# A finished token tile's layer norm recorded one step later, in a fused attention and feed-forward kernel

## The chip, the cores and the metric

The kernel runs on one core of a Trainium2 chip. The metric is the device time of one execution in microseconds (us). A profile of one further execution, taken by the hardware profiler, shows what every engine did: TensorE (PE, with its weight loads PEld), VectorE (DVE), ScalarE (ACT), GpSimd (POOL) and SyncE (SP, which here only issues transfers).

## The reference

Four batches, eight heads, 1152 positions of 64 elements. Queries are averaged in pairs of positions, so there are 576 rows of queries for each head. Attention is followed by a layer norm and a two-layer feed-forward part with a residual.

```python
q_pool = q.reshape(B, H, S // factor, factor, D).mean(axis=3)
scores = scale * np.matmul(q_pool, k.transpose(0, 1, 3, 2))
scores = scores - np.max(scores, axis=-1, keepdims=True)
attn = np.exp(scores)
attn = attn / (np.sum(attn, axis=-1, keepdims=True) + 1e-09)
attn_out = np.matmul(attn, v)
x = attn_out.transpose(0, 2, 1, 3).reshape(B, S, H * D)   # 4 x 576 x 512
xn = (x - mu) / np.sqrt(var + 1e-06) * g_ln
out = x + np.maximum(xn @ w_ch1, 0.0) @ w_ch2              # 512 -> 2048 -> 512
```

## The kernel before

**Steps.** A pair p is one batch and two heads; there are 16 pairs, and each has nine chunks of 128 query rows, so 144 steps. Step i takes the chunk i % 9 of pair i // 9 through a software pipeline that is written out by hand in `step(i)`. No scheduler reorders anything: each engine executes its instructions in the order in which the functions record them, and waits for the others by semaphores. In a step of batches 1 to 3 the order of recording is:

- VectorE's maximum of the scores (`emit_max`, L381) and the bias from it (L386);
- TensorE's scores of the next step (`emit_s(i + 1)`, L362 and L370), into one of two slots of three PSUM banks;
- `flush()`: the evacuations that were put off, on ScalarE and VectorE (`r` L513 and L514; kt and qt L286 and L283; ht L629 and L630; xn and xh L577 and L578);
- ScalarE's exp (L395, into a tile pe, two buffers) and the high half (`emit_hi`, L409, into hl, three buffers);
- `final`: ScalarE's evacuations L524 of the attention output into the token tile xb or xh, and behind each `evacuated(n)`, which counts how many chunks of the tile are there;
- the low half of step i - 1 (`emit_lo`): on VectorE as L418, or, in steps whose chunk is 2, 5 or 8, on GpSimd as L251 and L416; then SyncE's transposing transfer of hl into pt;
- `norm(i)`, at most one a step;
- the scales of the next pair (L232 to L242), when due;
- TensorE: attention times v (`a_piece`, L464), transposes of raw k or q (`a_prep`), one unit of the feed-forward part (`some_units`, L616 or L648), in an order that depends on whether transposes of a norm follow;
- what was booked for this step with `at(i, ...)`: among it the conversions of v on GpSimd (`take_v`, L251, L251, L278) and the transposes of a normalized tile (`ln_t`, L571).

Batch 0 runs in another form (`on_pe`), in which P is transposed on TensorE and VectorE evacuates the output.

**A norm.** A token tile is 128 tokens by 512, and it is whole when eight chunks have been evacuated into it. Then `evacuated` appends it to `norms`. `norm(i)` takes the first of them: `ln_a` records VectorE's statistics (L553, L554); `ln_r` records three small GpSimd operations (L559, L562, L563) and the normalization L565 into xs, on GpSimd while attention runs and on VectorE after. The four transposes of xs (L571, TensorE) are booked for step i + 2, or i + 1 once the steps of attention are over, and the feed-forward units for the step behind. A batch b has tiles (b, 0) to (b, 3); the fifth chunk of every pair makes half a tile, and two batches share such a half tile, h.

**PSUM.** Outside the two slots only banks 6 and 7 are free while attention runs. `bank()` hands them out in turn; a transposing group or a unit can only start when what was last in its bank has been evacuated by ScalarE and then VectorE.

Of the kernel before, what the change touches and what calls it, by code (L numbers as in the profile page):

```python
# [24 lines left out]
def tile_pooled_attention_moe(  # L25
# [23 lines left out]
    C = S // 128  # L49
    HP = H // 2  # L50
    NP = B * HP
    NSTEP = NP * C
# [44 lines left out]
    def drip(n=1):  # L97
        while n and (soon or fill):
            (soon or fill).popleft()()
            n -= 1  # L100
# [235 lines left out]
    def on_pe(i):  # L336

        return 0 <= i < HP * C
# [38 lines left out]
    def emit_max(i):  # L377
        st = steps[i]
        mx = sm_p.tile([128, 1], FP32, tag="mx", name="mx")
        nb = st["nb"] = sm_p.tile([128, 1], FP32, tag="nb", name="nb")  # L380
        nc.vector.tensor_reduce(mx, st["s"], axis=AX.X, op=ALU.max)  # L381
        sc = pair[i // C]["sc"]
        if on_pe(i):
            st["mx"] = mx
        else:
            nc.vector.tensor_scalar(nb, mx, sc[:, 0:1], -1.0, op0=ALU.mult, op1=ALU.mult)  # L386
# [44 lines left out]
    def emit_t_copy(i):  # L431
        st = steps[i]
        for a, b in ((0, 512), (512, S)):
            nc.scalar.copy(st["pt"][:, a:b], st["s"][:, a:b])
# [115 lines left out]
    def ln_a(st, x):  # L550
        bs = sm_p.tile([128, 6], FP32, tag="bs", name="bs")
        mv = sm_p.tile([128, 2], FP32, tag="mv", name="mv", bufs=5)
        nc.vector.bn_stats(bs, x)  # L553
        nc.vector.bn_aggr(mv, bs)  # L554
        st["x"], st["mv"] = x, mv

    def ln_r(st, eng):
        rs = sm_p.tile([128, 2], FP32, tag="rs", name="rs", bufs=2)
        nc.gpsimd.tensor_scalar(  # L559
            rs[:, 1:2], st["mv"][:, 1:2], 1e-6, 2.0 ** -4, op0=ALU.add, op1=ALU.mult  # L560
        )
        nc.gpsimd.tensor_scalar(rs[:, 0:1], st["mv"][:, 0:1], -1.0, 1.0, op0=ALU.mult, op1=ALU.mult)  # L562
        nc.gpsimd.tensor_tensor(rs[:, 1:2], rs[:, 1:2], nhalf, op=ALU.pow)  # L563
        xs = st["xs"] = x_p.tile([128, DM], FP32, tag="xs", name="xs")
        eng.tensor_scalar(xs, st["x"], rs[:, 0:1], rs[:, 1:2], op0=ALU.add, op1=ALU.mult)  # L565

    def ln_t(st, dst):

        ps = bank()
        for c in range(KD):  # L570
            nc.tensor.transpose(  # L571
                ps[:, 128 * c:128 * c + 128], st["xs"][:, 128 * c:128 * c + 128], ident
            )
        pv = ps.rearrange("p (c n) -> p c n", c=KD)
        hi, lo = dst[:, 0:KD], dst[:, KD:2 * KD]
        return (
            lambda: nc.scalar.copy(hi, pv),  # L577
            lambda: nc.vector.tensor_tensor(lo, pv, hi, op=ALU.subtract),  # L578
        )
# [5 lines left out]
    def until(fns, n=None):  # L585
        evacs.extend((n, fn) for fn in fns)
# [213 lines left out]
    def at(i, fn, *a):  # L800
        todo.setdefault(i, []).append((fn, a))
# [52 lines left out]
    this = [0]  # L854
# [10 lines left out]
                at(i0 + x, fn, 4 * part + n)  # L865


    norms, turns = deque(), set()
    room = {"xn": 2, "x": 8}
    batch = {}  # L870

# [24 lines left out]
    def norm(i):  # L896

        if not norms or norms[0][1] % 2 == 0 and norms[0][0] != "h" and not room["xn"]:
            return
        b, t = norms.popleft()  # L900
        st = {}
        if b == "h":
            x = xh[t][:, 0]
            dst = xh[t][:, 1].bitcast(FP16).rearrange("p (a n) -> p a n", a=2 * KD)
        else:
            x = xb[b][:, t]
            keep = batch.setdefault(b, {})
            if t % 2 == 0:
                keep["xn", t] = x_p.tile([128, 2 * KD, 256], FP16, tag="xn", name="xn")
                room["xn"] -= 1  # L910
            dst = keep["xn", t - t % 2][:, :, 128 * (t % 2):128 * (t % 2) + 128]
        ln_a(st, x)
        ln_r(st, nc.gpsimd if i < NSTEP else nc.vector)

        def transpose():
            until(ln_t(st, dst), nbank[1])

        d = 2 if i < NSTEP else 1
        at(i + d, transpose)
        turns.add(i + d)  # L920
        if b == "h":
            at(i + d + 1, units_of_half, t)
        elif t % 2:
            at(i + d + 1, units_of, b, t)
            if t == 3 and b == 1:
                at(i + d + 1, lambda: norms.append(("h", 0)))
# [3 lines left out]
    def evacuated(n):  # L930

        p, j = divmod(n, C)
        b = p // HP
        left[p] -= 1
        if not left[p]:
            pair.pop(p)
        key = ("h", b // 2) if j == 4 else (b, PLACES[p % HP // 2][j][1])
        whole[key] = whole.get(key, 0) + 1
        if whole[key] == 8 and key != ("h", 0):
            norms.append(key)  # L940

    left = [C] * NP
    ready = {}
# [4 lines left out]
    def a_prep():  # L948
        if preps:
            fn, p, u = preps.popleft()  # L950
            until(fn(p, u), nbank[1])
# [6 lines left out]
    def a_piece(i):  # L958
        pieces.extend(ready.pop(i, ()))
        for u in range(2 if len(pieces) > 2 and not on_pe(i) else 1):  # L960
            if pieces:
                n = pieces.popleft()
                pt = pts[n]
                ps = emit_pv(n, bank() if u or on_pe(n) else None)
                if on_pe(n):
                    ot = pt.rearrange("p a n -> p (a n)").bitcast(FP32)[0:65, 0:128]
                    until([lambda ot=ot, ps=ps: nc.scalar.activation(
                        out=ot, in_=ps[0:65, 0:128], func=ACTF.Identity, bias=eps
                    )], nbank[1])
                    turned.append((n, ot))  # L970
                    continue
                one, two = evac_pv(n, ps)
                until([one], nbank[1] if u else None)
                last.extend((two, lambda n=n: evacuated(n)))

    def step(i):
        live = i < NSTEP
        this[0] = i
        for fn, a in early.pop(i, ()):
            fn(*a)  # L980
        if live:
            emit_max(i)
        if on_pe(i - 1):
            emit_t_copy(i - 1)
            steps.pop(i - 1)
        while found:
            found.popleft()()
        first = on_pe(i - 2) or on_pe(i)
        final, last[:] = list(last), []
        if first and not on_pe(i):  # L990
            a_piece(i)
        if on_pe(i):
            if i < 3:
                warm(16, bank())
            a_piece(i)
            a_prep()
            emit_exp(i)
        while scaled_out:
            scaled_out.popleft()()
        if i + 1 < NSTEP:  # L1000
            emit_s(i + 1)
            pv_slot[0] = i + 1
        else:
            free_banks[:] = [6, 7, 0, 1, 3, 4]
            pv_slot[0] += 1
        if on_pe(i):
            while fill:
                drip()
            flush()
        else:  # L1010
            flush()
            if live:
                emit_exp(i)
                emit_hi(i)
        for fn in final:
            fn()
        if 0 <= i - 1 < NSTEP and not on_pe(i - 1):
            emit_lo(i - 1)
            steps.pop(i - 1)
            drip()  # L1020
        norm(i)
        red = None
        while soon or len(fill) > 3:
            drip()
        if on_pe(i):
            emit_t(i)
            if reds:
                found.append(reds.popleft()())
        elif reds:
            red = reds.popleft()  # L1030
            put = [None]
            until([lambda: put[0]()])
        while turned:
            n, ot = turned.popleft()
            emit_turn(n, ot, i)
        if not on_pe(i):
            if not first:
                a_piece(i)
            if red:
                put[0] = red()  # L1040
            if i in turns:
                a_prep()
            some_units(i)
            if i not in turns:
                a_prep()
        for fn, a in todo.pop(i, ()):
            fn(*a)
        if calm and i < HP * C - 1:
            gate()
        for _ in range(1 if i < HP * C - 1 else 2):  # L1050
            if calm:
                fn, n = calm.popleft()
                fn(n)

    def warm(n, ps=None):
        ps = psum[:, 2, 0:128] if ps is None else ps[:, 0:128]
        for _ in range(n):
            nc.tensor.matmul(out=ps, lhsT=ident16, rhs=ident16, start=True, stop=True)

    with tc.manual_schedule():  # L1060
# [47 lines left out]
        i = 0  # L1108
# [32 lines left out]
```

## Time and profile before

| | before |
|---|---|
| median of 3 runs | 849.92 us (846.39 to 850.97) |
| profiled execution, its own time | 847.87 us |
| its span, first to last instruction | 846.1 us |
| TensorE busy | 812.0 us (96%) |
| VectorE busy | 599.8 us (71%) |
| ScalarE busy | 557.6 us (66%) |
| GpSimd busy | 351.4 us (42%) |
| mean granted TensorE clock | 0.989 |

The busy share of an engine is an average over all stages. Idle time of an engine is put down to the event that ended it; it costs something only where the work that waited is itself waited for, in the end by the engine that ends last. The granted clock is 1 at 2.4 GHz and 0.5 at 1.2 GHz.

### The profile page before, as it was taken

What the parts mean: (1) busy time and instruction counts of PE and PEld (TensorE: products, weight loads), DVE (VectorE), ACT (ScalarE), POOL (GpSimd) and SP (SyncE); (2) the same over time, 40 slices, a digit from 0 to 9 for tenths busy, and PEclk for the clock granted to TensorE, in tenths of its full rate; (3) what the DMA queues carried; (4) which work ended last, traced back from release to release, by engine and by line L of the source; (5) the groups of instructions that cost most, each with busy time, mean ns of one, the idle gap of its engine ahead of it and who ended that gap; (6) DMA issues with size and microseconds to landing.
All of it is one profiled execution on the core that took longest, in us unless ns stands there. A gap on an engine that the chain in (4) does not pass through costs nothing.

```text
span 846.1 us, 21643 instructions
## 1 busy us (share of the span) xinstructions
PE 812.0 (96%) x9142; PEld 577.8 (68%) x9142; DVE 599.8 (71%) x1166; ACT 557.6 (66%) x810; POOL 351.4 (42%) x345
## 2 busy tenths in 40 slices
PE   8999999988989999998999999999999999999997
PEld 6787878766656675656675766676766767766764
DVE  3698989887857888787787877878787877522221
ACT  3999998876666776786686868686778676311110
POOL 3020234395997964546434244635543422300000
PEclk9999999999999999999999999999999999999999
DMA  6853475024697879888899989787979777501001
GB/s 164 242 184 134 151 206 174 12 60 85 130 205 119 181 133 218 167 174 145 146 195 164 174 151 211 146 154 144 214 145 189 136 133 119 110 2 26 14 1 25
DMA packets 276018, 115.96 MB, mean 137 GB/s; under 512 B 259281, under 2 KB 259281, under 8 KB 275921
## 3 DMA queue, kind: packets, MB, share of 16 engines
q1 hardware_dynamic: 275568, 113.70, 65.8%
q8 instruction: 71, 1.16, 0.6%
q10 hardware_dynamic: 352, 0.88, 0.4%
q14 instruction: 27, 0.21, 0.1%
HBM read 46.14 MB, written 4.72 MB: 60 GB/s over the span
## 4 chain that ended last, share of the span: by engine, by line
PE 57%; DVE 12%; ACT 11%; DMA 9%; issue 5%; POOL 3%; SPq 2%; ACTq 0%; POOLq 0%; DVEq 0%
PE psum L648 17%; PE psum L616 17%; PE psum L464 7%; PE psum L362 6%; DMA pt<-hl 5%; ACT pe L395 4%; DVE mx L381 3%; PE psum L452 2%; PE psum L370 2%; DMA kr<-in_k_dram 2%; DMA qr<-in_q_dram 2%; PE psum L428 1%; PE psum L325 1%; ACT kt L185 1%; DVE hl L418 1%
## 5 line engine op out<-in xcount | busy, mean ns | idle before, releaser
L381 DVE TENSOR_REDUCE mx<-psum 128x1 f32<-128x1152 f32 x144 | 194.4, 1350 | 19.2 <-PE psum L464 4.7
L395 ACT ACTIVATE pe<-psum,nb,sc 128x1152 f32<-128x1152 f32 x144 | 188.5, 1309 | 15.2 <-DVE r L513 9.4
L648 PE MATMUL psum<-wsl,ht 128*128 128x512 f16 x864 | 196.7, 379 | 0.2 <-ACT pe L395 0.2
L616 PEld LDWEIGHTS <-wsl 128*128 128x128 f16 x1920 | 170.8, 98 | 21.8 <-issue 2.0
L616 PE MATMUL psum<-xn,wsl 128*128 128x256 f16 x1536 | 179.5, 275 | 1.3 <-DVE ht L630 0.6
L648 PEld LDWEIGHTS <-ht 128*128 128x128 f16 x864 | 80.5, 98 | 88.3 <-issue 0.2
L409 ACT ACTIVATE hl<-pe 128x1152 f16<-128x1152 f32 x108 | 125.6, 1163 | 12.6 <-DMA pt<-hl 9.5
L629 ACT ACTIVATE ht<-psum 128x512 f16<-128x512 f32 x72 | 42.8, 595 | 132.6 <-PE psum L616 130.8
L362 PE MATMUL psum<-kt,qt 64*128 64x512 f16 (+1 forms) x960 | 127.8, 381 | 0.7 <-ACT pe L395 0.5
L464 PE MATMUL psum<-vt,pt 128*128 128x65 f16 (+1 forms) x3240 | 117.7, 194 | 0.0
L464 PEld LDWEIGHTS <-pt 128*128 128x128 f16 (+1 forms) x3240 | 109.3, 101 | 2.9 <-issue 0.2
L630 DVE SCALAR_TENSOR_TENSOR ht<-psum,ht 128x512 f16<-128x512 f32 x72 | 49.6, 689 | 83.9 <-ACT ht L629 83.7
L418 DVE SCALAR_TENSOR_TENSOR hl<-pe,hl 128x1152 f16<-128x1152 f32 x72 | 107.4, 1491 | 0.0
L251 POOL TENSOR_SCALAR pe<-pe 128x1152 f32<-128x1152 f32 x36 | 43.2, 1199 | 118.1 <-ACT hl L409 109.2
L416 POOL TENSOR_TENSOR hl<-pe,hl 128x1152 f16<-128x1152 f32 x36 | 85.5, 2374 | 3.0
L452 PE MATMUL psum<-pt,vt 128*65 128x128 f32 (+1 forms) x720 | 78.8, 265 | 1.9 <-DVE qt L283 1.9
L452 PEld LDWEIGHTS psum<-pt,vt 128*65 128x65 f32 x720 | 73.0, 140 | 2.2 <-DVE qt L283 2.2
L362 PEld LDWEIGHTS <-qt 64*128 64x128 f16 (+1 forms) x960 | 39.9, 97 | 38.2 <-issue 22.0
L370 PEld LDWEIGHTS <-qt 128*128 128x128 f16 (+1 forms) x320 | 17.5, 99 | 67.9 <-issue 67.7
L257 POOL COPY gate<-gate 128x1 f32<-128x1 f32 x27 | 5.2, 191 | 111.0 <-DVE gate L256 111.0
L662 DVE SCALAR_TENSOR_TENSOR xb<-psum,inv,xb 128x512 f32<-128x512 f32 x32 | 23.9, 747 | 37.3 <-PE psum L648 37.0
L283 DVE SCALAR_TENSOR_TENSOR qt<-psum,s,qt 128x384 f16<-128x384 f32 x48 | 29.4, 614 | 29.0 <-ACT qt L286 28.8
(116 smaller groups left out, 1020.4 us busy)
## 6 DMA issues: line engine op xcount, KB each, us to landing
stage<-in_moe_w_ch_dram SPq DMA_DIRECT2D x32, 512.0 KB, 5.8
kr<-in_k_dram SPq DMA_DIRECT2D x16, 576.0 KB, 4.5
qr<-in_q_dram SPq DMA_DIRECT2D x31, 288.0 KB, 6.3
vr<-in_v_dram SPq DMA_DIRECT2D x15, 576.0 KB, 4.9
out_dram<-xb SPq DMA_DIRECT2D x32, 128.0 KB, 2.5
pt<-hl SPq DMA_TRANSPOSE x108, 5.0
kr<-in_k_dram SPq DMA_DIRECT2D x16, 64.0 KB, 4.2
vr<-in_v_dram ACTq DMA_DIRECT2D x1, 576.0 KB, 6.4
```

The costliest lines, as they stand in the source:

```text
L251: nc.gpsimd.tensor_scalar(dst, src, s, 1.0, op0=ALU.mult, op1=ALU.mult)
L362: nc.tensor.matmul(out=sp[o:o + w, c0:c0 + 512], lhsT=qt[r:r + 64, qa, q0:q0 + w], rhs=kt[r:r + 64, ka, h], start=(a == 0), stop=(a == 2),)
L381: nc.vector.tensor_reduce(mx, st["s"], axis=AX.X, op=ALU.max)
L395: nc.scalar.activation(out=st["pe"], in_=st["s"], func=ACTF.Exp, scale=pair[i // C]["sc"][:, 0:1], bias=st["nb"],)
L409: nc.scalar.activation(out=hl[:, 0], in_=st["pe"], func=ACTF.Copy, scale=2.0 ** 15)
L416: nc.gpsimd.tensor_tensor(hl[:, 1], st["pe"], hl[:, 0], op=ALU.subtract)
L418: nc.vector.scalar_tensor_tensor(hl[:, 1], st["pe"], 2.0 ** 15, hl[:, 0], op0=ALU.mult, op1=ALU.subtract)
L452: nc.tensor.matmul(out=ps[0:65, q0:q0 + w], lhsT=vt[:, h, c], rhs=pt[:, 128 * u + q0:128 * u + q0 + w], start=(u == 0), stop=(u == C - 1),)
L464: nc.tensor.matmul(out=dst[:, 0:n], lhsT=lhsT, rhs=rhs, start=(u == 0 and lhsT is hi and n == 65), stop=(u == C - 1 and lhsT is lo), skip_ ...
L616: nc.tensor.matmul(out=ps[:, o:o + n], lhsT=wsl[:, 8 * w + cc, wa, f * 128:f * 128 + 128], rhs=xn[:, xa * KD + cc, 0:n], start=(m == 0), s ...
L630: lambda: nc.vector.scalar_tensor_tensor(lo, pv, 0.0, hi, op0=ALU.max, op1=ALU.subtract),
L648: nc.tensor.matmul(out=ps, lhsT=hv[0][:, ha, f, t * 128:t * 128 + 128], rhs=wsl[:, 8 * w + 4 + f // 2, wa, (f % 2) * DM:(f % 2) * DM + DM] ...
```

## The change

The change keeps two lists of whole tiles. A tile that becomes whole through an evacuation on ScalarE (every tile of batches 1 to 3 that is whole before step 144, and half tile 1 at step 144) goes to `fresh`, which is appended to `norms` only behind `norm(i)`; its norm is thus recorded in step i + 1. The transposes of a norm that is recorded in step 63 or later are booked one step behind it instead of two, so that those of the moved tiles stay in their step. Half tile 0, whose norm stays in step 80, gets its transposes in step 81 instead of 82, and half tile 1, whose norm moves from step 144 to 145, gets them in 146 instead of 145. All else on TensorE keeps its place, apart from the raw q transposes and the unit of step 81, which change places. SyncE's order is the same throughout.

```diff
--- before.py
+++ after.py
@@ -865,7 +865,7 @@
                 at(i0 + x, fn, 4 * part + n)
 
 
-    norms, turns = deque(), set()
+    norms, fresh, turns = deque(), deque(), set()
     room = {"xn": 2, "x": 8}
     batch = {}
 
@@ -915,7 +915,7 @@
         def transpose():
             until(ln_t(st, dst), nbank[1])
 
-        d = 2 if i < NSTEP else 1
+        d = 2 if i < 2 * HP * C - C else 1
         at(i + d, transpose)
         turns.add(i + d)
         if b == "h":
@@ -937,7 +937,7 @@
         key = ("h", b // 2) if j == 4 else (b, PLACES[p % HP // 2][j][1])
         whole[key] = whole.get(key, 0) + 1
         if whole[key] == 8 and key != ("h", 0):
-            norms.append(key)
+            (norms if on_pe(n) or this[0] >= NSTEP else fresh).append(key)
 
     left = [C] * NP
     ready = {}
@@ -1019,6 +1019,8 @@
             steps.pop(i - 1)
             drip()
         norm(i)
+        norms.extend(fresh)
+        fresh.clear()
         red = None
         while soon or len(fill) > 3:
             drip()
```

Two places follow in the recorded order. VectorE in step 76, with the low half of step 75 in the first row, the scales of pair 9 (L232 to L242) and kt of pair 9 in the last. Before:

```order
L418 SCALAR_TENSOR_TENSOR hl<-pe,hl 128x1152
L553 BN_STATS bs<-xb 128x6
L554 BN_AGGR mv<-bs 128x2
L232 TENSOR_SCALAR red<-psum 128x3
L237 TENSOR_SCALAR e<-red 128x3
L238 TENSOR_SCALAR s<-red 128x3
L240 TENSOR_SCALAR s<-s 128x3
L242 SCALAR_TENSOR_TENSOR sc<-e 128x1
L513 TENSOR_SCALAR r<-psum,s 128x1
L514 RECIPROCAL r<-r 128x1
L283 SCALAR_TENSOR_TENSOR kt<-psum,s,kt 128x512
```

After:

```order
L418 SCALAR_TENSOR_TENSOR hl<-pe,hl 128x1152
L232 TENSOR_SCALAR red<-psum 128x3
L237 TENSOR_SCALAR e<-red 128x3
L238 TENSOR_SCALAR s<-red 128x3
L240 TENSOR_SCALAR s<-s 128x3
L242 SCALAR_TENSOR_TENSOR sc<-e 128x1
L513 TENSOR_SCALAR r<-psum,s 128x1
L514 RECIPROCAL r<-r 128x1
L283 SCALAR_TENSOR_TENSOR kt<-psum,s,kt 128x512
```

The statistics of tile (1, 3), L553 and L554, have left this place; they stand behind the L418 of the next step.

GpSimd in steps 74 to 76: L559 to L565 is a norm, L251 and L416 the low half of step 74. Before, with the norm of tile (1, 2) first:

```order
L559 TENSOR_SCALAR rs<-mv 128x1
L562 TENSOR_SCALAR rs<-mv 128x1
L563 TENSOR_TENSOR rs<-rs,nhalf 128x1
L565 TENSOR_SCALAR xs<-xb,rs 128x512
L251 TENSOR_SCALAR pe<-pe 128x1152
L416 TENSOR_TENSOR hl<-pe,hl 128x1152
```

After:

```order
L251 TENSOR_SCALAR pe<-pe 128x1152
L416 TENSOR_TENSOR hl<-pe,hl 128x1152
L559 TENSOR_SCALAR rs<-mv 128x1
L562 TENSOR_SCALAR rs<-mv 128x1
L563 TENSOR_TENSOR rs<-rs,nhalf 128x1
L565 TENSOR_SCALAR xs<-xb,rs 128x512
```

The low half of step 74 now stands ahead of the norm of tile (1, 2). Where no low half lies between the two steps, the norm stays in its place among GpSimd's instructions.

## Rows read from the trace of the kernel before

**Rows 1.** The page, part 1: busy us, share, instructions.

```profile
PE 812.0 (96%) x9142; PEld 577.8 (68%) x9142; DVE 599.8 (71%) x1166; ACT 557.6 (66%) x810; POOL 351.4 (42%) x345
```

**Rows 2.** Who waited for whom, whole run: us in total, times, longest.

```profile
DVE bs L553 <- ACT xb L524: 9.6, 9, 1.9
ACT hl L409 <- DMA pt<-hl: 9.5, 9, 2.8
...
PE psum L370 <- ACT xb L524: 5.4, 4, 2.7
...
PE psum L571 <- DVE kt L283: 3.4, 2, 2.4
```

**Rows 3.** Timeline, steps 74 to 77: start, us, engine, line, operation, [idle before <-releaser].

```profile
379.39 1.16 ACT L409 ACTIVATE hl<-pe 128x1152 f16<-128x1152 f32 x1
...
380.78 0.69 DVE L553 BATCH_NORM_STATS2 bs<-xb 128x6 f32<-128x512 f32 x1 [0.59 <-ACT xb L524]
...
383.41 1.31 ACT L395 ACTIVATE pe<-psum,nb,sc 128x1152 f32<-128x1152 f32 x1 [1.37 <-DVE r L513]
...
383.60 1.15 POOL L251 TENSOR_SCALAR pe<-pe 128x1152 f32<-128x1152 f32 x1
...
384.83 2.37 POOL L416 TENSOR_TENSOR hl<-pe,hl 128x1152 f16<-128x1152 f32 x1
...
386.17 0.27 PE L370 MATMUL psum<-kt,qt 128*128 128x128 f16 x2 [0.34 <-ACT xb L524]
...
387.24 1.31 ACT L395 ACTIVATE pe<-psum,nb,sc 128x1152 f32<-128x1152 f32 x1 [0.64 <-POOL hl L416]
387.24 1.35 DVE L418 SCALAR_TENSOR_TENSOR hl<-pe,hl 128x1152 f16<-128x1152 f32 x1
...
389.98 0.69 DVE L553 BATCH_NORM_STATS2 bs<-xb 128x6 f32<-128x512 f32 x1 [1.39 <-ACT xb L524]
...
391.51 0.69 ACT L286 ACTIVATE kt<-psum,s 128x512 f16<-128x512 f32 x1 [1.56 <-DVE s L240]
...
392.08 0.77 POOL L565 TENSOR_SCALAR xs<-xb,rs 128x512 f32<-128x512 f32 x1
...
392.23 0.75 DVE L283 SCALAR_TENSOR_TENSOR kt<-psum,s,kt 128x512 f16<-128x512 f32 x1 [0.43 <-ACT kt L286]
...
393.13 0.63 PE L571 MATMUL psum<-ident,xs 128*128 128x128 f32 x4 [2.36 <-DVE kt L283]
...
394.57 1.25 POOL L278 TENSOR_TENSOR vt<-vr,vt 128x576 f16<-128x576 f32 x1
```

**Rows 4.** Stretches: length, busy PE, PEld, DVE, ACT, POOL, clock, DMA, GB/s.

```profile
332.00:340.00 8.00, 5.80 (x96) 4.51 (x95) 5.74 (x11) 6.84 (x10) 3.84 (x3) 1.00 1.15 229
...
393.20:397.00 3.80, 3.80 (x43) 2.65 (x44) 3.77 (x6) 3.03 (x4) 2.43 (x3) 0.62 0.32 62
```

**Rows 5.** Timeline, step 72, TensorE.

```profile
368.65 0.63 PE L571 MATMUL psum<-ident,xs 128*128 128x128 f32 x4 [0.37 <-DVE qt L283]
```

**Rows 6.** Timeline, steps 111 to 113, TensorE.

```profile
565.22 2.84 PE L616 MATMUL psum<-xh,wsl 128*128 128x128 f16 x48 [0.28 <-DVE xh L662]
...
574.48 0.63 PE L571 MATMUL psum<-ident,xs 128*128 128x128 f32 x4 [1.05 <-DVE kt L283]
```

**Rows 7.** Timeline, step 143, TensorE.

```profile
721.00 2.75 PE L648 MATMUL psum<-wsl,ht 128*128 128x512 f16 x12 [0.25 <-ACT pe L395]
```

**Rows 8.** Timeline, steps 78 to 81.

```profile
398.36 2.37 POOL L416 TENSOR_TENSOR hl<-pe,hl 128x1152 f16<-128x1152 f32 x1
...
406.05 1.31 ACT L395 ACTIVATE pe<-psum,nb,sc 128x1152 f32<-128x1152 f32 x1
...
410.14 0.82 PE L362 MATMUL psum<-kt,qt 64*128 64x512 f16 x6
```

**Rows 9.** Timeline, step 64, GpSimd and VectorE.

```profile
328.45 2.62 POOL L166 TENSOR_TENSOR qr<-qr 128x1152 f32<-128x1152 f32 x1 [2.99 <-DMA qr<-in_q_dram]
...
328.89 3.39 DVE L418 SCALAR_TENSOR_TENSOR hl<-pe,hl 128x1152 f16<-128x1152 f32 x1
```

## The prediction

> **What bounds the kernel now.** I read the page first: TensorE is busy 812.0 of 846.1 us [rows 1], so at most 34 us are to be had from waits, and only waits that end at TensorE count. The view of who waited for whom comes next. VectorE waits 9.6 us in nine places for ScalarE's evacuation L524 before the statistics of a norm, L553; TensorE's waits include 3.4 us in two places at the transposes L571 for VectorE's kt, L283 [rows 2]. The timeline around those places tells whether the first kind causes the second. Steps are counted by VectorE's maxima L381, the first being step 0.
>
> Steps 74 to 77 [rows 3]. At 380.78 the statistics of tile (1, 2) start after 0.59 us of waiting, and what is queued behind them on VectorE, the maximum of step 75, starts late; ScalarE then idles 1.37 us before the exp at 383.41. GpSimd is hit too: its norm operations stood ahead of the pair L251, L416 of step 74, so that the pair starts only at 383.60 and ends at 387.20, and the exp of step 76 at 387.24 waits 0.64 for it. TensorE waits 0.34 at 386.17. At 389.98 the statistics of tile (1, 3) have cost VectorE 1.39 us of waiting and 0.69 of work; behind them stand the scales of the next pair, ScalarE's kt at 391.51 (idle 1.56) and L283 at 392.23, which frees the PSUM bank; TensorE's transposes start at 393.13, 2.36 us late. Just behind that wait the granted clock is 0.62 over 3.8 us, that is, part of the stretch at 1.2 instead of 2.4 GHz: 3.8 x 0.38 = 1.44 us of clock lost [rows 4]. The transposes of step 112 repeat the pattern at 574.48 with 1.05 us, an L616 at 565.22 has 0.28, and the transposes of step 71, at 368.65, have 0.37 [rows 5, 6].
>
> **The change part by part.** It adds no work: ten norms (all tiles of batches 1 and 2, two of batch 3) and, pushed along, the one of half tile 1 stand one step later on VectorE and GpSimd. TensorE's order stays, but for two groups of four transposes. SyncE's queue stays.
>
> *The wait goes.* One step on, L524 has long run, so the nine waits fall. The statistics' 0.69 and their small aggregate remain and stand behind the next step's low part instead.
>
> *Step 75.* Without statistics in step 74, VectorE ends L418 by 380.20 and takes the maximum of step 75 at once, 1.4 us earlier. The exp at 383.41 had ScalarE free since 382.04, so it gains 1.37. Everything behind it on ScalarE moves along, L524 too, and TensorE's 0.34 at 386.17 is gone.
>
> *Step 76.* GpSimd's pair runs right behind ScalarE's hi of step 74, L409 (ended 380.55), so 3.0 earlier, and no longer holds the exp of step 76, which comes about 1.5 earlier, at 385.7; ScalarE is through hi of step 76 at 385.7 + 1.31 + 1.16 = 388.2 and through L524 by 388.5. VectorE's L418, at 386.4 behind ht, ends at 387.7, the five scale operations are through by 388.4, ScalarE's kt runs 388.5 to 389.2 and L283 ends at 390.0. TensorE comes to L571 at 393.13 - 2.36 = 390.77, or 390.06 once the earlier 0.37 and 0.34 are counted; of the chain before L571 the parts that wait for TensorE shift with it. So 2.36 go to nothing, with about half a microsecond to spare, and with the wait the slow stretch goes: in the stretch 332 to 340 TensorE was busy only 5.80 of 8.00 us, in shorter waits, and the clock stayed at 1.00 [rows 4]; behind the 2.36 in one piece it did not. Worth 1.44, bounds 0 and 1.44.
>
> *The other three.* At 368.65 the transposes wait for an L283 that stood behind the statistics of (1, 1), whose 0.69 exceed the 0.37. At 574.48 the L283 stood behind those of (2, 3), 0.69 and a wait that is one of the nine; together they exceed the 1.05. The 0.28 at 565.22 hangs on an L662 that came behind the maximum of step 111, itself behind the statistics of (2, 2). All three go, 1.70 [rows 5, 6].
>
> *Step 142.* The statistics of (3, 0) stand between L418 and the maximum of step 143, which pushes that maximum by 0.15 or so; TensorE already waits 0.25 for the exp of that step [rows 7]. I count -0.15.
>
> *Half tile 0.* Its transposes move from step 82 to step 81, where they need the bank that prep_q has just filled, as those of step 71 did. That bank is emptied by ScalarE and VectorE while TensorE is busy with 12 L648 (2.75 us in [rows 7]); I get qt done at 420.9 and TensorE there at 420.9. Cost 0, bounds 0 and 0.37, the wait at 368.65.
>
> *The tail.* From step 144 TensorE never waits, and its work is the same. Tile (3, 1) now has its norm where half tile 1 had it, and its xs is ready no later than the 730.4 that half tile 1 reached; cost 0.
>
> Sum: 0.37 + 0.34 + 2.36 + 1.44 + 0.28 + 1.05 - 0.15 = 5.7 us. Against the profiled execution's own 847.87 that is 842.2; that execution lies 2.05 under the median of the three runs, 849.92, and the same gain on the median gives **844.2**. Of TensorE's 34 us not busy, hardly any lies from 78 to 111 or from 114 on, so what is gained at 77 and 113 should stay gained.
>
> *What is late next.* GpSimd in step 77. Before, its norm was over before the three conversions of v, and its pair of step 77 ended at 398.36 + 2.37 = 400.73. Now the statistics come behind L418 of step 76, at 393.7; xs follows 2.9 later (as 389.98 to 392.85), the conversions take 3.0 (as 392.85 to 395.82), the pair 3.5 (1.15 + 2.37): it ends at 403.1. The exp of step 79 writes the buffer that this pair reads; with all shifted by 4.5 it would start at 406.05 - 4.5 = 401.55, so it waits 1.55 and ends at 404.4. TensorE's scores of step 81 need it at 410.14 - 4.5 = 405.6 [rows 3, 8]: 1.2 us of cover remain. The shift of 4.5 is 0.37 + 0.34 + 2.36 + 1.44. Step 113 is the same, with less shift.
>
> On that place bears a row of the present trace: L418 took 3.39 us at 328.89 where 1.35 is usual, beside a GpSimd operation of 2.62 us that had begun at 328.45 [rows 3, 9]: it was held 2.04. The Trainium skill, "SBUF — State Buffer", section "Who interferes with whom", says that a VectorE instruction with two SBUF inputs and a GpSimd instruction that reads SBUF exclude each other for the whole instruction. The trace agrees (2.04 us held). By that rule the later GpSimd work meets an L418 more often, and each meeting would take up to 2.04 from the 1.2 us of cover; where none meets, the sum stays 5.7.
>
> **The rivals.** *The clock does not come back, or half the wait remains* (B). The window at 1.2 GHz opens anyway, or L571 waits another microsecond because kt needs ScalarE, which is free at 388.5 only by my timing. For it: the spare half microsecond is thinner than my rounding. Gain 5.7 - 1.44 = 4.3: 845.7.
>
> *The wait changes hands* (C). L283 is as late as before, since ScalarE's own queue is as long as VectorE's. Against it: ScalarE stood idle 1.56 ahead of the kt, waiting for VectorE's scales, and VectorE had waited 1.39 and worked 0.69 for the statistics just ahead of them. Left would be 0.37 + 0.34 + 0.28 = 1.0: 848.9.
>
> *GpSimd becomes the wait* (D, slower). At steps 77 and 113 the pair is held once, 2.04; beyond the cover of 1.2 TensorE waits 0.84 at step 81, and the transfer of the pair's result holds ScalarE's next hi, as nine times before (up to 2.8), so that L370 waits up to 2.7 for L524 [rows 2], and the clock falls for 1.44. That is 5.0 a place, 10.0 in all: 849.92 - 5.7 + 10.0 = 854.2. It decides from the point where the pair of step 77 ends later than TensorE's scores of step 81 less one exp. For it: the rule above and three GpSimd jobs in a row. Against it: it needs a meeting at both places, and beyond 1.2 us of cover each time.
>
> **How the numbers follow.** Forecast (A) 0.55, around 844.2, its own range 842.0 to 846.0; B 0.22; C 0.15; D 0.08. About 0.5%, 4.25 us, is what a measurement of this kernel can tell from no change, so the border lies at 845.7: most of A (0.50) and half of B (0.11) are faster, the rest of A, half of B and C are the same, and D is slower with a little of C's spread. Faster 0.61, same 0.31, slower 0.08. The range takes in A, B and C with the runs' own spread of some 2 us: 841.0 to 849.8; D and what is beyond lie outside.
>
> **What would show it.** In the profile after: no wait of L553 for L524; the transposes of steps 76 and 112 without a wait for kt; granted clock 1.00 in the 7 us behind the first of them; the exp of step 75 without its 1.37. A pair L251, L416 that ends only where the exp of step 79 is due would show the GpSimd step right, and a TensorE wait at steps 80 to 82 that it isn't covered. L571 waiting still for kt would be C. A total above 847 with all waits gone would say that the time comes back in the stretch from 78 to 111.

## The result, and the profile after

| | before | after |
|---|---|---|
| median of 19 runs each | 846.39 us (843.24 to 850.97) | 851.45 us (848.46 to 854.3) |
| span of the profiled execution | 846.1 us | 847.4 us |
| mean granted TensorE clock | 0.989 | 0.992 |

The ratio of the times is 1.0054, 95% interval 1.0041 to 1.0068: the change makes the kernel slower by 0.54%, some 4.6 us, where 0.67% faster was forecast, and the 851.45 lies outside the forecast's range of 841.0 to 849.8. The median of the three runs of before that the forecast stood on, 849.92, lies 3.5 us above that of the nineteen.

TensorE is as busy as before, but for 1.3 us in 812 [rows 1]. First the page's row, then the view of who waited for whom, of the kernel after (us in total, times, longest):

```profile
PE 810.7 (96%) x9142; PEld 576.4 (68%) x9142; DVE 600.7 (71%) x1167; ACT 557.2 (66%) x810; POOL 354.5 (42%) x344
```

```profile
ACT hl L409 <- DMA pt<-hl: 17.6, 17, 2.9
...
POOL qr L166 <- DMA qr<-in_q_dram: 15.1, 4, 6.1
...
PE psum L370 <- ACT xb L524: 8.3, 7, 2.5
...
PE psum L201 <- ACT kt L185: 5.4, 5, 1.7
...
ACT pe L395 <- POOL hl L416: 3.2, 2, 1.6
```

VectorE's nine waits for L524 and TensorE's two for VectorE's kt [rows 2] are no longer in this view: what the change set out to remove is removed. In their place ScalarE waits 17.6 us instead of 9.5 for the transposing transfers that read hl, TensorE 8.3 instead of 5.4 for L524, and GpSimd 15.1 instead of 8.7 us for q loads.

**Where TensorE gains and loses.** TensorE's order is the same in both kernels up to one swap in step 81, so the start of the first L464 of a step tells how far it is. The table takes these starts from the traces; a difference between two stretches is what was gained or lost in between.

| first L464 of | before | after | after minus before | change since the row above |
|---|---|---|---|---|
| step 71 | 364.03 | 361.15 | -2.88 | |
| step 78 | 400.74 | 392.89 | -7.85 | -4.97 |
| step 85 | 435.90 | 430.44 | -5.46 | +2.39 |
| step 101 | 514.15 | 508.68 | -5.47 | -0.01 |
| step 103 | 523.65 | 519.81 | -3.84 | +1.63 |
| step 111 | 563.84 | 559.98 | -3.86 | -0.02 |
| step 113 | 575.91 | 570.38 | -5.53 | -1.67 |
| step 118 | 601.55 | 596.01 | -5.54 | -0.01 |
| step 121 | 614.96 | 616.55 | +1.59 | +7.13 |
| step 143 | 718.86 | 720.45 | +1.59 | 0.00 |

So 6.6 us are gained where the forecast had them (4.97 and 1.67), and 11.2 are lost: 2.4 behind step 78, 1.6 at step 102, 7.1 behind step 118. The -2.88 ahead of step 71 isn't put down to the change: a kernel below that is unchanged up to step 77 lies 4.87 ahead at the same point. What is compared is the part from step 71 to step 143: +4.5 us, about what the times show.

**The gain.** Steps 76 to 78 in the timeline of after (start, duration, engine, line; in brackets the idle time before and what ended it), to be read against [rows 3]:

```profile
386.83 0.63 PE L571 MATMUL psum<-ident,xs 128*128 128x128 f32 x4
...
390.58 0.69 DVE L553 BATCH_NORM_STATS2 bs<-xb 128x6 f32<-128x512 f32 x1
...
391.56 0.19 POOL L559 TENSOR_SCALAR rs<-mv 128x1 f32<-128x1 f32 x1 [8.83 <-DVE mv L554]
...
397.11 0.63 PE L571 MATMUL psum<-ident,xs 128*128 128x128 f32 x4
...
397.58 2.37 POOL L416 TENSOR_TENSOR hl<-pe,hl 128x1152 f16<-128x1152 f32 x1
...
399.99 1.31 ACT L395 ACTIVATE pe<-psum,nb,sc 128x1152 f32<-128x1152 f32 x1 [1.62 <-POOL hl L416]
```

The statistics wait for nothing. The transposes at 386.83 are those that waited 2.36 us at 393.13 before; they and the next ones, at 397.11, wait for nothing either. GpSimd's pair of step 77 ends at 399.95 (397.58 + 2.37), and the exp of step 79 waits 1.62 us for it: the forecast said 1.55. TensorE did not wait at step 81 for that exp, as forecast.

**The loss.** GpSimd's pair of step 113 and SyncE's own queue in the two traces, from the transfer of that pair's result to the q loads behind it (L421 is a transposing transfer of hl to pt, L667 a store of the output, L131 a load of q; a duration is the time that SyncE is at it, and a row with x2 runs from the start of the first transfer to the end of the second). The second transfer of the first L421 row is the pair's in both. Before, then after:

```profile
579.71 2.37 POOL L416 TENSOR_TENSOR hl<-pe,hl 128x1152 f16<-128x1152 f32 x1
...
578.51 6.26 SPq L421 DMA_TRANSPOSE pt<-hl  x2
586.13 1.13 SPq L667 DMA_DIRECT2D out_dram<-xh  x2
588.10 3.26 SPq L421 DMA_TRANSPOSE pt<-hl  x1
591.41 2.51 SPq L131 DMA_DIRECT2D qr<-in_q_dram  x4
594.08 5.21 SPq L421 DMA_TRANSPOSE pt<-hl  x1
```

```profile
579.40 2.37 POOL L416 TENSOR_TENSOR hl<-pe,hl 128x1152 f16<-128x1152 f32 x1
...
572.60 12.76 SPq L421 DMA_TRANSPOSE pt<-hl  x2
585.40 1.23 SPq L667 DMA_DIRECT2D out_dram<-xh  x2
586.79 2.72 SPq L421 DMA_TRANSPOSE pt<-hl  x1
589.56 2.51 SPq L131 DMA_DIRECT2D qr<-in_q_dram  x4
592.23 5.81 SPq L421 DMA_TRANSPOSE pt<-hl  x1
```

At this point TensorE is 5.5 us earlier than before, but the pair ends only 0.3 us earlier (581.77 against 582.08). Its transfer can't start sooner, SyncE is busy from there without a pause over 0.2 us, and the q loads come only 1.85 us earlier (589.56 against 591.41). A transposing transfer keeps SyncE some 2.7 to 3.3 us (586.79 after, 588.10 before), and 5 to 6 us behind the q loads. Behind them the transfers come too late for ScalarE, which can write the next hl only when the transfer that reads the old one has landed. Timeline of after, the three steps behind:

```profile
598.30 2.61 POOL L166 TENSOR_TENSOR qr<-qr 128x1152 f32<-128x1152 f32 x1 [6.07 <-DMA qr<-in_q_dram]
...
600.16 1.16 ACT L409 ACTIVATE hl<-pe 128x1152 f16<-128x1152 f32 x1 [2.93 <-DMA pt<-hl]
...
601.58 0.27 PE L370 MATMUL psum<-kt,qt 128*128 128x128 f16 x2 [1.21 <-ACT xb L524]
...
602.63 1.16 ACT L185 ACTIVATE kt<-kr 128x1152 f16<-128x1152 f32 x1 [1.10 <-DMA kr<-in_k_dram]
...
605.62 0.84 PE L362 MATMUL psum<-kt,qt 64*64 64x512 f16 x12 [0.36 <-ACT pe L395]
...
606.55 1.16 ACT L409 ACTIVATE hl<-pe 128x1152 f16<-128x1152 f32 x1 [0.98 <-DMA pt<-hl]
...
607.97 0.30 PE L370 MATMUL psum<-kt,qt 128*64 128x128 f16 x4 [1.50 <-ACT xb L524]
...
610.26 0.38 PE L201 MATMUL psum<-ident,acc 128*3 128x128 f32 x1 [0.84 <-ACT kt L185]
610.43 5.32 PE L648 MATMUL psum<-wsl,ht 128*128 128x512 f16 x12
```

L524 stands behind hi on ScalarE, and L370 needs the bank that L524 empties: 1.21 and 1.50 us. With 0.36 for an exp and 0.84 for a kt that came late, TensorE idles 3.9 us. The clock falls behind the third of these waits, ahead of the fourth. Busy time by stretch of the kernel after (the number before the DMA share is the granted clock):

```profile
386.00:393.00 7.00, 6.96 (x85) 4.97 (x83) 6.89 (x11) 4.82 (x7) 1.25 (x4) 1.00 0.64 119
600.00:608.00 8.00, 4.92 (x59) 2.62 (x57) 3.56 (x5) 5.76 (x9) 2.26 (x3) 1.00 1.06 251
609.00:615.00 6.00, 5.16 (x20) 2.04 (x18) 2.25 (x6) 5.60 (x8) 2.44 (x2) 0.50 1.02 193
610.00:617.00 7.00, 6.74 (x36) 2.56 (x37) 3.40 (x8) 5.45 (x8) 1.48 (x2) 0.60 0.77 145
```

In the first stretch, where before had 0.62 [rows 4], the clock is full. From 600 to 608 it still is; from 609 to 615 it is 0.50, that is 1.2 GHz. The twelve L648 at 610.43 took 5.32 us, where before has 2.75 for them at 611.40. These 2.6 us and some 0.6 in the matmuls around them make up, with the 3.9, the 7.1 of the table.

Behind step 78 there are three waits, 0.55, 0.62 and 0.73 us (419.58, 421.29 and 426.73), and the granted clock stays at 1.00 from 410 to 430: the loss there is 2.4 and not 7.1.

### The profile page after: what moved, and what is told of

It reads as the page before. It is cut to its first block, busy times and chain, and to the rows that moved or that the text cites. A ratio compares the mean times of both kernels' runs of the same rounds, so it can differ in the third digit from the quotient of the medians.

```text
span 847.4 us, 21642 instructions
## 1 busy us (share of the span) xinstructions
PE 810.7 (96%) x9142; PEld 576.4 (68%) x9142; DVE 600.7 (71%) x1167; ACT 557.2 (66%) x810; POOL 354.5 (42%) x344
## 4 chain that ended last, share of the span: by engine, by line
PE 60%; ACT 10%; DVE 9%; DMA 9%; POOL 6%; issue 4%; SPq 2%; POOLq 0%; ACTq 0%; DVEq 0%
PE psum L616 19%; PE psum L648 17%; PE psum L464 8%; PE psum L362 6%; ACT pe L395 4%; DVE mx L381 3%; PE psum L452 3%; DMA qr<-in_q_dram 2%; DMA pt<-hl 2%; PE psum L370 2%; PE psum L428 2%; DMA kr<-in_k_dram 1%; ACT kt L185 1%; DMA vr<-in_v_dram 1%; POOL hl L416 1%
## 5 line engine op out<-in xcount | busy, mean ns | idle before, releaser
L648 PE MATMUL psum<-wsl,ht 128*128 128x512 f16 x864 | 199.2, 383 | 0.0
L616 PE MATMUL psum<-xn,wsl 128*128 128x256 f16 x1536 | 177.6, 274 | 1.4 <-DVE xb L662 0.8
L648 PEld LDWEIGHTS <-ht 128*128 128x128 f16 x864 | 81.1, 98 | 89.7 <-issue 2.7
L409 ACT ACTIVATE hl<-pe 128x1152 f16<-128x1152 f32 x108 | 125.6, 1163 | 20.5 <-DMA pt<-hl 17.6
L464 PE MATMUL psum<-vt,pt 128*128 128x65 f16 (+1 forms) x3240 | 117.2, 193 | 0.0
L464 PEld LDWEIGHTS <-pt 128*128 128x128 f16 (+1 forms) x3240 | 108.8, 100 | 2.6 <-issue 0.2
L418 DVE SCALAR_TENSOR_TENSOR hl<-pe,hl 128x1152 f16<-128x1152 f32 x72 | 108.6, 1509 | 0.0
L251 POOL TENSOR_SCALAR pe<-pe 128x1152 f32<-128x1152 f32 x36 | 42.1, 1170 | 124.8 <-ACT hl L409 124.8
L416 POOL TENSOR_TENSOR hl<-pe,hl 128x1152 f16<-128x1152 f32 x36 | 85.5, 2374 | 3.0
L370 PEld LDWEIGHTS <-qt 128*128 128x128 f16 (+1 forms) x320 | 17.9, 99 | 70.3 <-issue 70.1
```

The lines of the kernel that those rows point to most:

```text
L409: nc.scalar.activation(out=hl[:, 0], in_=st["pe"], func=ACTF.Copy, scale=2.0 ** 15)
L416: nc.gpsimd.tensor_tensor(hl[:, 1], st["pe"], hl[:, 0], op=ALU.subtract)
L418: nc.vector.scalar_tensor_tensor(hl[:, 1], st["pe"], 2.0 ** 15, hl[:, 0], op0=ALU.mult, op1=ALU.subtract)
L464: nc.tensor.matmul(out=dst[:, 0:n], lhsT=lhsT, rhs=rhs, start=(u == 0 and lhsT is hi and n == 65), stop=(u == C - 1 and lhsT is lo), skip_ ...
L616: nc.tensor.matmul(out=ps[:, o:o + n], lhsT=wsl[:, 8 * w + cc, wa, f * 128:f * 128 + 128], rhs=xn[:, xa * KD + cc, 0:n], start=(m == 0), s ...
L648: nc.tensor.matmul(out=ps, lhsT=hv[0][:, ha, f, t * 128:t * 128 + 128], rhs=wsl[:, 8 * w + 4 + f // 2, wa, (f % 2) * DM:(f % 2) * DM + DM] ...
```

## Experiments

Four questions: which of the moved norms loses the time; whether GpSimd's late pair is the cause; what carries it to TensorE; and whether the gain stays once that is mended. Ratios are to the kernel before, run on the same chip beside it, with 95% intervals.

### Which norms

**e1_half_back.** The transposes of half tile 0 go back to step 82.

```diff
-    norms, fresh, turns = deque(), deque(), set()
+    norms, fresh, turns, moved = deque(), deque(), set(), set()
...
-        d = 2 if i < 2 * HP * C - C else 1
+        d = 2 if i < NSTEP and (b, t) not in moved else 1
...
-            (norms if on_pe(n) or this[0] >= NSTEP else fresh).append(key)
+            late = not on_pe(n) and this[0] < NSTEP and (True)
+            (fresh if late else norms).append(key)
+            if late:
+                moved.add(key)
```

> The changed kernel with one part undone: the transposes of half tile 0 stay in step 82, as before; the eleven norms stay one step later. Theory G (GpSimd's late pair of steps 77 and 113 holds SyncE's queue, the q loads behind it come late, and ScalarE's high half waits for a transposing transfer): no change against the changed kernel, about 851, and the waits of L370 around steps 82 to 84 and 119 to 121 stay. Theory H (the half tile's transposes, squeezed into step 81 behind a full bank, cost the time): back to 846 or below. Theory N (what TensorE gains anywhere is lost again in the next stretch with q loads, since the transfers set the pace there): about 851.

849.88 us, ratio 1.0038 (1.0022 to 1.0055): still slower, so the half tile is not the cause.

**e2_last_only** and **e3_all_but_last.** As e1, but of the ten norms only the last tile of batch 1 and of batch 2 move, in steps 76 and 112, or all but these two.

```diff
-            late = not on_pe(n) and this[0] < NSTEP and (True)
+            late = not on_pe(n) and this[0] < NSTEP and (key[1] == 3)   # e2; e3: != 3
```

> The kernel before, with the norms of tiles (1, 3) and (2, 3) alone moved a step later (from 76 to 77 and from 112 to 113), transposes in their old steps. Theory G: the whole loss is here, 850 to 853, and the high half's waits for transposing transfers rise from 9.5 us towards 17 us. Theory H: 844 to 846, since two of the removed waits of TensorE (2.36 and 1.05 us) are gone and nothing is squeezed. Theory N: 846 to 848, gained and given back.

> The changed kernel without what the run of two norms has: all moved norms but those of (1, 3) and (2, 3) stay a step later, these two are back in steps 76 and 112, half tile 0 as before. Theory G: no loss, 844 to 847, SyncE issues the transfer of the pair of steps 77 and 113 about as early as before. Theory H: the same, since the half tile is back. Theory N: 848 to 851, since the exp of step 75 and the GpSimd pair of step 74 still come earlier and the time is lost at the next q loads.

e2: 850.86 us, 1.0059 (1.0035 to 1.0083). e3: 842.97 us, 0.9966 (0.9947 to 0.9984), a little better than the 844 to 847 that theory G expected. Theory N, that any gain is lost again at the next q loads, falls with e3. The whole loss comes with these two norms, the ones whose new place is just ahead of GpSimd's pair of steps 77 and 113; the other eight are worth 0.34%.

### Is it GpSimd's pair

**e4_stats_early.** All ten move, but VectorE's statistics are recorded right behind the maximum of the next step, ahead of its low part, so that GpSimd gets them sooner; the normalization stays.

```diff
+        norms.extend(fresh)
+        if fresh:
...
+            b, t = fresh.popleft()
+            done.append({})
+            ln_a(done[0], xh[t][:, 0] if b == "h" else xb[b][:, t])
...
-        ln_a(st, x)
+        if not done:
+            ln_a(st, x)
+        else:
+            st.update(done.pop())
```

> All eleven norms a step later, but VectorE's two statistics operations stand right behind the maximum and its bias of that step instead of behind the low half; GpSimd's order as in the changed kernel, half tile 0 as before. In step 77 GpSimd's norm can then start about 2.5 us earlier and the pair behind the v conversions too. Theory G: half of the loss or more is gone, 846 to 849. Theory H: 846 or below, since the half tile is back. Theory N: about 851.

845.77 us, 0.9995 (0.9976 to 1.0014). The pair of step 77 ends 9.08 us behind the start of its hi, where it was 4.86 before and 10.37 after: little of the lateness is gone, and some of the loss with it. The time alone, just below theory G's range, would fit theory H too; it was e1 that ruled out H.

**e5_pair_on_dve.** As e1, but the low parts of steps 77 and 113 are VectorE's L418 instead of GpSimd's pair.

```diff
-        return i % C in (2, 5, 8)
+        return i % C in (2, 5, 8) and i not in (77, 113)
```

> All eleven norms a step later, half tile 0 as before, and the low halves of steps 77 and 113 computed by VectorE (one L418 of 1.35 us) instead of GpSimd's pair behind the norm and the v conversions. Theory G (the late pair, and with it SyncE's queue, costs the time): the waits of L370 near steps 83 to 85 and 119 to 121 go, and the removed waits of TensorE show: 841 to 844. Theory N2 (it is VectorE's statistics standing behind the low half of steps 76 and 112 that cost, by a later maximum): VectorE gets 1.35 us more in the next step, so 850 or more.

841.09 us, 0.9958 (0.9938 to 0.9978). With the late pair gone, the gain is there. This also rules out that the moved statistics cost by a later maximum on VectorE: they stand where they stood in e1.

**e6_gpsimd_held.** The reverse: the kernel before, no norm moved, and GpSimd held at the start of steps 77 and 113 by 36 writes of a scratch tile that nothing reads.

```diff
+    junk = const.tile([128, 64], FP32, name="junk")
...
+    def hold():
+        for _ in range(36):
+            nc.gpsimd.memset(junk, 0.0)
+    pre(77, hold)
+    pre(113, hold)
```

> The kernel before, no norm moved, but GpSimd executes 36 small memsets of a scratch tile, about 5 us in all, ahead of the v conversions of steps 77 and 113; so its pair of these steps is some 4 us later and nothing else changes. Theory G: the late pair alone costs what the change lost and more, since nothing is gained: 850 to 856, with the same waits of the high half near steps 82 and 118. Theory N2: GpSimd's lateness is covered, 845 to 847.

854.87 us, 1.0130 (1.0096 to 1.0164). The writes took 7.46 us where about 5 were planned. Its timeline, with every line number higher by one: the pair of step 77 (L417) ends 10.7 us behind the start of its hi (L410 at 392.23), and the waits of the changed kernel stand behind step 118, on the same instructions:

```profile
388.93 7.46 POOL L857 MEMSET junk<- 128x64 f32 x36
...
392.23 1.16 ACT L410 ACTIVATE hl<-pe 128x1152 f16<-128x1152 f32 x1
...
400.57 2.38 POOL L417 TENSOR_TENSOR hl<-pe,hl 128x1152 f16<-128x1152 f32 x1
```

```profile
602.64 2.62 POOL L167 TENSOR_TENSOR qr<-qr 128x1152 f32<-128x1152 f32 x1 [5.67 <-DMA qr<-in_q_dram]
604.40 1.16 ACT L410 ACTIVATE hl<-pe 128x1152 f16<-128x1152 f32 x1 [3.42 <-DMA pt<-hl]
605.82 0.27 PE L371 MATMUL psum<-kt,qt 128*128 128x128 f16 x2 [1.71 <-ACT xb L525]
...
612.51 0.30 PE L371 MATMUL psum<-kt,qt 128*64 128x128 f16 x4 [1.65 <-ACT xb L525]
```

A late pair is enough to make the loss, without any moved norm.

### What carries it

**e7_q_ahead.** As e1, with the pair left late on GpSimd, but the q loads of the two pairs concerned are issued two steps sooner, so that they stand ahead of the late transfer in SyncE's queue.

```diff
-                at(i0 - 2, load_q, p, (nc.sync,))
+                at(i0 - (4 if p in (10, 14) else 2), load_q, p, (nc.sync,))
```

> All eleven norms a step later, half tile 0 as before, and SyncE issues the q loads of pairs 10 and 14 two steps earlier, ahead of the transfer of the late pair and of the two behind it. Theory G with SyncE's queue as the carrier (the late transfer and the q loads behind it pile up): most of the loss goes, 843 to 847. Theory G with GpSimd itself as the carrier (the pe buffer, or VectorE's L418 held beside the pair): about 850, as without it.

839.42 us, 0.9932 (0.9907 to 0.9958), better than the 843 to 847 expected. SyncE's queue around step 77 (the row at 402.74 begins with the late pair's transfer) and the view of who waited for whom, of this kernel:

```profile
393.55 2.68 SPq L421 DMA_TRANSPOSE pt<-hl  x1
396.27 2.51 SPq L131 DMA_DIRECT2D qr<-in_q_dram  x4
402.74 8.94 SPq L421 DMA_TRANSPOSE pt<-hl  x3
```

```profile
ACT hl L409 <- DMA pt<-hl: 9.5, 10, 2.7
...
POOL qr L166 <- DMA qr<-in_q_dram: 5.6, 2, 2.9
...
PE psum L370 <- ACT xb L524: 4.2, 3, 1.8
...
ACT pe L395 <- POOL hl L416: 3.2, 2, 1.6
```

The exp still waits 3.2 us in two places for the late pair, as in the changed kernel; ScalarE's waits for the transfers are back at 9.5. So the pair's direct wait costs TensorE nothing, and the order in SyncE's queue is what turns it into a loss.

**e8_q_ahead_before.** The control: the same two loads sooner in the kernel before.

> The control to the run before it: the kernel before, no norm moved, with the q loads of pairs 10 and 14 two steps earlier. Nothing waits there before, so both forms of theory G expect 845 to 847, no change; if it gains as much as the run before it, the q loads' place is a cost of its own and has nothing to do with the moved norms.

845.17 us, 0.9995 (0.9976 to 1.0013). The loads alone gain nothing, the moved norms alone lose, both together gain 0.68%.

**e10_after_q_ahead.** The changed kernel itself, half tile included, with the same edit of the two loads.

> The changed kernel as it is, half tile included, with the q loads of two pairs issued two steps sooner as in e7_q_ahead. It differs from e7 by the half tile's transposes alone, which stand in step 81 here and in step 82 there. The theory that the half tile costs nothing: 839 to 840 us, ratio 0.991 to 0.995, and no idle time of TensorE at steps 83 to 85 and 119 to 121. The theory that it costs what the first experiment hinted (849.88 beside 851.45, 0.15%): 840.5 to 842 us, ratio 0.994 to 0.997.

840.38 us, 0.9950 (0.9933 to 0.9967). TensorE has no wait over 0.3 us at steps 83 to 85 or 119 to 121. Its ratio lies in the range of the second theory, while the waits are gone as the first expected. Its interval and e7's overlap, and in the table below e10 loses nothing where the half tile's transposes stand: a cost of the half tile can't be told from none.

### Does the queue cost elsewhere too

**e9_q_ahead_all**, **e11_q_ahead_all_before**, **e12_q_ahead_pair_on_dve.** The q loads of all five pairs that are loaded this way two steps sooner: with e1's moved norms; in the kernel before; and with e5's low parts on VectorE as well.

```diff
-                at(i0 - 2, load_q, p, (nc.sync,))
+                at(i0 - 4, load_q, p, (nc.sync,))
```

> The changed kernel with the half tile's transposes back in their old step, and with the q loads of every pair whose q is loaded this way issued two steps sooner on SyncE's queue (e7_q_ahead did so for the two pairs behind steps 77 and 113 alone: 839.42 us, ratio 0.993). If SyncE's queue gives back gains only where a late transfer of step 77's or 113's kind stands ahead of the loads, the other three pairs have nothing to give: ratio 0.991 to 0.995, 838 to 841 us, and TensorE idles for the transposes of q at the other pairs as before. If any pair's loads stand late in this queue, the waits of GpSimd for q (5.6 us in e7) and TensorE's idle time of 0.40 us at step 102 fall as well: ratio 0.988 to 0.992. If the earlier loads at the other pairs push a transposing transfer behind them, ScalarE's waits for pt rise above e7's 9.5 us and the ratio is above 0.995.

> The kernel before with the q loads of all five pairs issued two steps sooner on SyncE's queue: what this edit is worth without the moved norms. With them it took the kernel from 0.993 (two pairs) to 0.990 (all five), and in that trace TensorE's idle time at steps 48 and 65 and the slow clock at step 49 were gone. If that further 0.3% is the loads' own, this kernel shows it alone: ratio 0.995 to 0.998, with the idle time at steps 48 and 65 gone and that at step 77 (2.4 us) still there. If the loads pay only together with the moved norms, the ratio is 0.999 to 1.001, as for the two pairs alone.

> Both cures at once: q loads of all pairs two steps sooner, and the low parts of steps 77 and 113 on VectorE instead of GpSimd. If the two cures remove the same loss (GpSimd's late pair costs only through what it delays on SyncE's queue), the second adds nothing: ratio 0.988 to 0.993, as with the loads alone (0.990). If the late pair also costs by ScalarE's exp that waits for it (L395 waits for L416: 3.2 us in two places with the loads moved), the ratio falls by 0.2 to 0.4% more: 0.985 to 0.988.

e9: 836.11 us, 0.9904 (0.9880 to 0.9928). e11: 840.41 us, 0.9948 (0.9930 to 0.9966). e12: 836.64 us, 0.9901 (0.9882 to 0.9919). The kernel before already lost some 0.5% to late q loads at other pairs. Steps 48 and 49 show it: timeline of e8, where the loads of that pair stand as before, then of e9, and one stretch behind it in each:

```profile
245.38 1.16 ACT L409 ACTIVATE hl<-pe 128x1152 f16<-128x1152 f32 x1 [2.11 <-DMA pt<-hl]
246.79 0.30 PE L370 MATMUL psum<-kt,qt 128*64 128x128 f16 x4 [1.68 <-ACT xb L524]
249.08 0.38 PE L201 MATMUL psum<-ident,acc 128*3 128x128 f32 x1 [1.06 <-ACT kt L185]
```

```profile
249.00:256.00 7.00, 6.92 (x68) 5.07 (x69) 4.78 (x9) 5.61 (x8) 6.83 (x5) 0.78 0.93 156
```

```profile
247.59 1.16 ACT L409 ACTIVATE hl<-pe 128x1152 f16<-128x1152 f32 x1 [1.16 <-DMA pt<-hl]
251.30 0.27 PE L201 MATMUL psum<-ident,acc 128*3 128x128 f32 x1 [0.65 <-ACT kt L185]
```

```profile
251.00:258.00 7.00, 6.70 (x79) 5.44 (x80) 6.00 (x10) 5.65 (x9) 6.92 (x5) 1.00 0.51 110
```

The wait of L370 is gone and the clock stays at 1.00. No norm is moved that early, and e11 has no wait of L370 there either. The second cure adds nothing to the first (e12 beside e9), so both remove the same loss. e9 and e12 beat the kernel before by 1%, and the changed one by more.

### All runs in one table

TensorE's gain (-) or loss (+) in us against before, from the starts of L464 as above, one profiled execution each:

| kernel | steps 47 to 71 | 71 to 78 | 78 to 85 | 101 to 103 | 111 to 113 | 118 to 121 | 71 to 143 in all |
|---|---|---|---|---|---|---|---|
| after | -2.2 | -5.0 | +2.4 | +1.6 | -1.7 | +7.1 | +4.5 |
| e1, half tile back | -2.1 | -4.2 | +4.6 | +0.1 | -1.7 | +6.3 | +5.1 |
| e2, last two only | -2.7 | -3.2 | +5.0 | -0.1 | -1.2 | +5.1 | +5.6 |
| e3, all but these | -1.2 | -3.4 | 0.0 | +0.5 | -0.4 | 0.0 | -3.4 |
| e4, statistics early | -2.9 | -4.5 | +4.1 | +0.1 | -1.7 | +5.0 | +3.2 |
| e5, pair on VectorE | -2.2 | -4.2 | +0.1 | 0.0 | -1.7 | +0.5 | -5.3 |
| e6, before, GpSimd held | -2.2 | -0.1 | +1.2 | +0.8 | 0.0 | +6.7 | +8.8 |
| e7, two loads sooner | -0.9 | -4.0 | -0.1 | +0.1 | -1.7 | 0.0 | -5.7 |
| e8, the same in before | -3.0 | 0.0 | -0.3 | 0.0 | 0.0 | 0.0 | -0.4 |
| e10, the same in after | -2.3 | -4.5 | +0.1 | +0.1 | -1.7 | 0.0 | -6.1 |
| e9, all loads sooner | -6.3 | -5.1 | -0.1 | -0.4 | -1.7 | 0.0 | -7.3 |
| e11, the same in before | -6.8 | 0.0 | -0.3 | -0.4 | 0.0 | 0.0 | -0.7 |
| e12, both cures | -5.0 | -4.4 | +0.1 | -0.4 | -1.7 | 0.0 | -6.4 |

The first column holds up to 3 us that come and go (e8 changes nothing there and shows -3.0); the others repeat within a few tenths where nothing is changed. Reading down: the kernels that lose behind steps 78 and 118 are those with a late pair and the old loads (after, e1, e2, e4, e6); no other loses more than 0.5 there.

## Why the prediction was wrong

- **"The wait goes", "Step 75", "Step 76", "The other three": right.** The nine waits are gone. Up to step 78 the sum was 4.5, measured 4.97 in after and 4.0 to 5.1 in the others that move all ten norms; at step 112 it was 0.28 + 1.05 = 1.33, measured 1.67. The 1.44 for the clock was read from a stretch that ends inside the slow one: from 393 to 400 before has 0.76 of 7 us, 1.7 lost. The clock is back at 1.00 behind L571. Rivals B and C fall.
- **"What is late next": the step that failed.** Its timing held: the wait of 1.62 against 1.55 forecast, and no wait of TensorE for that exp. But the step ended at "1.2 us of cover remain", that is, it followed the late pair only to the exp that reuses that pair's buffer. The pair has a second successor, the transposing transfer of its result on SyncE's queue, and with it all that is queued behind: the q loads, then the transfers of the next steps. "SyncE's queue stays" was true of its order and said nothing of its times. The step was costed at 0; it cost 2.4 us behind step 78 and 7.1 behind step 118, and e7, which keeps the pair as late (10.4 us behind the start of its hi) and moves only loads in that queue, loses nothing at either place.
- **"Step 113 is the same, with less shift"** was wrong in size: the loss there is three times that at step 77, since TensorE's waits are longer there (3.9 us against 1.9) and the clock falls among them.
- **"What is gained at 77 and 113 should stay gained"** fell with it: it rested on TensorE's small idle time there before the change, which says nothing of how close the engines behind it are to being late. The last signpost of the prediction, a total above 847 with all waits gone, came true, but only 4.0 of the 11.2 us were lost in the stretch that it named, from 78 to 111.
- **Step 142, half tile 0, the tail: right to a few tenths.** The table has 0.00 from step 121 to step 143 in after. The 0.15 counted at step 143 had the wrong sign: TensorE's wait of 0.25 at 721.00 [rows 7] did not grow but is gone in after. Of the half tile e10 shows no cost that can be told from none. (Half tile 1 is whole only in step 144, so the code sends it to `norms`, not to `fresh`; its norm moves because that of (3, 1) stands ahead of it, as the prediction has it.)
- **Rival D** had the place, the carrier's last links (transfer, hi, L524, L370, clock) and nearly the size (4.3 us slower, measured 4.6), at a chance of 0.08. The size is luck: it counted 5.0 at each place, and the two cost 2.4 and 7.1. Its trigger was another, a VectorE L418 that meets a GpSimd operation at both places. That did happen once: L418 took 3.57 us at 415.17 in after, beside L166 of 2.63 us that had begun at 414.89, 2.2 more than its usual 1.35. The Trainium skill, "SBUF — State Buffer", section "Who interferes with whom", has two such instructions exclude each other for the whole instruction, and this row agrees. Of TensorE's waits only the 0.62 us for VectorE at 421.29 may hang on it, which no run isolates. In after no such meeting stands at steps 113 to 121, where most of the loss is, so it does not decide.
- **Left open:** the 1.6 us of after at step 102. They end at a kt (L185) that waited for loads of k and v, in the same queue, but no other kernel with the late pair shows them at this size (0.8 at most, in e6), and no run isolates them.

With the queue mended, the change is worth about what the sum said: -5.7 us in e7's trace from step 71 to 143, -0.68% in its time. That this meets the forecast 5.7 to the tenth is chance: the parts are 0.5 below and 0.3 above it, and e5 and e10, where the loss is gone or nearly so, have -5.3 and -6.1 us, -0.42% and -0.50%.

## What to carry to other kernels

When a step makes one engine's result later, follow it to every reader, and where a reader is an in-order queue of transfers, to everything queued behind it: an unchanged order can still shift loads by microseconds. Put loads that nobody has to produce ahead of transfers that wait for an engine. And align two traces by the starts of an engine whose order is the same in both: the differences by stretch show a gain and its loss separately, where the total shows only their sum.

## What was not expected of the hardware

- A transposing transfer of 128 x 2304 fp16 kept SyncE 2.72 us (586.79 in after), and 5.2 to 6.2 us when it stood behind four q loads of 288 KB (5.21 at 594.08 in before; 5.81 at 592.23 and 6.22 at 408.47 in after).
- TensorE's granted clock was 1.00 from 600 to 608 us of after and 0.50 from 609 to 615, behind three short waits (1.21, 0.36 and 1.50 us), none of them as long as the 2.36 us in one piece of before [rows 3]. Behind waits of 0.55, 0.62 and 0.73 us it stayed at 1.00 (410 to 430).
